# Sinkhorn attention and a two-layer feed-forward: four more groups of batch 0 compute their scores twice, with a new instruction order

## The chip, the cores and the metric

The kernel runs on one core of one Trainium2 chip. The time is the device time of an execution in microseconds (us); where several executions were timed, the median is given. Within the core, five engines work side by side, each through its own list of instructions in order: PE (TensorE, the matrix multiplier, with its weight loads shown as PEld), DVE (VectorE), ACT (ScalarE), POOL (GpSimd) and SP (SyncE, which here only starts transfers). PE writes to PSUM, eight banks; DVE and ACT read it from there.

## The reference

q, k, v are (4, 8, 768, 64): batch, head, token, feature. The 768 tokens of a head are 8 blocks of 96.

```
P = sort_net                                   # (4, 8, 8, 8)
for _ in range(5):
    P = exp(P - max(P, -1)); P /= sum(P, -1) + 1e-9; P /= sum(P, -2) + 1e-9
k_sorted = einsum('bhij,bhjcd->bhicd', P, k_blocks);  v_sorted likewise
scores = q_block @ k_sorted_block.T / sqrt(64)          # 96 x 96 inside each block
attn = exp(scores - max(scores, -1)); attn /= sum(attn, -1) + 1e-9
x = (attn @ v_sorted), heads side by side               # 3072 tokens x 512
h = x @ w_in                                            # 512 -> 2048
g = max(h, 0) + alpha * min(h, 0)
out = g @ w_out                                         # 2048 -> 512, f32
```

The scale 1/8 is folded into the matrix that sorts the keys.

## The kernel before

The whole computation is written as a list of 1158 operations, each with what it reads and writes. A table `ORDER` then gives, engine by engine, the order in which the operations stand; a number such as `480` is an operation, and `4.2` means four filler matmuls (128x512, line 1006) into bank 2, whose result nobody reads. A second table, `BANKS`, gives the PSUM banks. `emit` adds a semaphore wait wherever an operation needs another engine's result. So the two tables alone set the order of the work; nothing is decided at run time, and an engine whose next instruction has to wait holds back everything behind it.

The work has these parts:

- The Sinkhorn loop on 32x64 numbers (lines 546 to 560), DVE and ACT in turn. It ends with `Pb`, which is spread (`spread0`, line 569) into the sorting matrices `BDK` and `BDV`. Meanwhile PE runs 226 tiny matmuls (line 899) and 12 fillers (line 1006), which need `identb` (an identity that ACT copies from `identf`).
- Preparation of each batch. q is transposed (batch 0 on PE, line 434, and copied out to `QT`; later batches by conversion to `QI` and a transposing transfer). Keys are sorted by matmul (line 634 for batch 0, line 656 later, from `KSz`, which POOL or DVE fill at line 644) and copied to `KT`. Values are first rearranged within `VST` by copies on POOL, ACT or DVE, then sorted (lines 680, 701) and copied out to `VS`. Most of these copies go through one helper, line 395.
- Attention in 32 groups, group g being block g % 8 of batch g // 8, all 8 heads at once. A string `STYLE`, one letter to a group, chooses how the exponentials get to be laid out with keys on the partitions, as the next product needs them:
  - all styles: 8 matmuls for the scores with queries on the partitions (line 736) and a DVE reduction for minus the row maxima, to `nf` in f32 or `nm` in bf16 (line 740);
  - `t`: ACT takes the exponential in 8 instructions, one to a head, the maximum as bias (`Esb`, line 764); PE transposes it (8 matmuls, line 775); ACT or DVE copies the result to `ET` (line 395);
  - `f`: the same 8 instructions, and a transposing transfer from `Esb` to `ET` on SP's queue (line 784);
  - `n`: PE computes the scores again, this time with keys on the partitions (8 matmuls, line 748), then adds minus the maxima of each query by 8 matmuls of the broadcast `nm` with the identity (line 756), and ACT takes the exponential of all 768 columns in one instruction straight to `ET` (line 790).
  
  The product with the values (line 800), the division by the row sums (`rec`, `xq`, lines 806, 809) and the transposition to `xT` (line 823 on PE for groups 0 to 13, line 816 on SP later) are common to all.
- The feed-forward, in 9 chunks of groups (`CHUNKS`: groups 0-1, 2-3, then four at a time). First layer: line 844 on PE, relu(-h) to `t` on ACT (line 851), and `hT` on DVE (line 855). Second layer: line 877, 128 tokens at a time, in four parts of four matmuls each; parts 0 and 1 read the first half of `w_out_bf`, parts 2 and 3 the second. Its result is copied to `outstg` and stored by SP.

All loads go through POOL's queue; a half of `w_out_bf` is loaded by each of the two instructions at line 931, a batch's q by line 417, its keys by line 467, its values by line 477.

The lines that choose between the styles, in `attention`:

```
nx, nk_ = (nf[m], ("nf", m)) if st != "n" else (nm[m], ("nm", m))
...
else:
    G.add(PE, s2, 175, r=kt_keys + qt_keys + [("nm", m)], w=[X], prio=prio + 0.04, mode=2)
    G.add(PE, sub, 8 * 43, r=[("nm", m), "identb"], w=[X], prio=prio + 0.04)
    G.add(ACT, lambda e: e.activation(
        AP(ET[me], 0, [[800, 96], [384, 2], [1, 384]]),
        AP(ps, X.at(), [[LP, 96], [X.step, 2], [1, 384]]),
        ACTF.Exp), 810, r=[X], w=[("ET", me)], prio=prio + 0.05)
```

Of the kernel before, what the change touches and what calls it, by code (L numbers as in the profile page):

```python
# [29 lines left out]
LP_K = {1: 4.6, 2: 9, 3: 16}  # L30
LP_V = {0: 0.5, 1: 4.8, 2: 12, 3: 12.1}
PRQ = {1: 6, 2: 13, 3: 20}
STYLE = 'nntttttt' + 'f' * 24
XPE = range(14)
NWI = 2
CHUNKS = [(0, 2), (2, 4), (4, 8), (8, 12), (12, 16), (16, 20), (20, 24), (24, 28), (28, 32)]
# [3 lines left out]

ORDER = {
    "pool": """
# [3 lines left out]
        635 636 681 680 639 638 683 637 682 792 737 823 643 736 822 645 641""",  # L46
    "sync": """
        0 5 144 146 142 339 386 401 436 381 377 379 468 268 495 529 566 598 644 649 675 623 365 570 705 602 729 562
        519 759 679 642 701 653 665 787 709 640 733 817 841 791 869 777 763 895 921 821 845 873 746 941 856 813 967
        1019 945 925 954 899 993 917 885 983 1039 997 971 1052 1023 1043 1015 1073 1118 1097 1157 1139 1145 1151""",  # L50
    "pe": """
# [14 lines left out]
        1094 1116 1119 1152 1135 1140 1128 1125 1136 1095 1141 1137 1142 1153 1154 1155 1146 1143 1147 1148 1149""",  # L66
    "act": """
# [8 lines left out]
        1078 1075 1081 1087 1084 1099 1102 1108 1123 1132 1090 1105 1117 1120 1111 1126 1129 1096 1150""",  # L76
    "dve": """
# [13 lines left out]
        1091 1106 1121 1112 1130 1127 1156 1138 1144""",  # L91
}
BANKS = (
    "0620452304660313015574545676716120235015223234367260175607327340012372454015406160154561306612014745"
    "2372547711223545052501562444232357714015607641707623454050002063014560754074271564560372340127266560"
    "1352511234767505012321670645230525760101427573401234475010153772230155166122341043423245312323046000"
    "15625371235600260123354164151324667144620334051605"
)


# [218 lines left out]
def bass_sinkhorn_attn__then__act_prelu_kernel(  # L319
# [393 lines left out]
    def attention(g, prio):  # L713
        b, i = g // NB, g % NB
        n, m, me = b % 2, g % 2, g % NE
        st = STYLE[g]
        kt_keys = [("KT", n, u) for u in range(6)]
# [328 lines left out]
```

## Time and profile before

| | |
|---|---|
| median of 3 runs | 238.45 us (237.95 to 238.58) |
| the profiled execution | 237.39 us, of which the profile's span is 235.7 us |
| PE busy | 221.9 us (94%) |
| DVE, ACT, POOL busy | 174.8 us (74%), 156.5 us (66%), 82.8 us (35%) |
| moved by transfers | 29.17 MB, mean 124 GB/s |

The profiled execution is 1.06 us below the median; 1.69 us of it lie outside the span. Times in the profile's views count from the span's start. A busy PE includes the time in which a matmul runs through the array, so short gaps between matmuls do not show as idle.

### The profile page before, as it was taken

Reading aid. Unit: us, or ns where it says so; the run is one execution under the profiler, and the core shown is the slowest. Engines: PE = TensorE matmul, PEld = TensorE weight load, DVE = VectorE, ACT = ScalarE, POOL = GpSimd, SP = SyncE. Lnnn points to the kernel's source line nnn. Section 1 sums busy time; section 2 is a strip of 40 time slices with the busy share of each in tenths; the row PEclk is TensorE's granted clock in tenths of the full one; section 3 lists DMA queues with packets and bytes.
Section 4 is the critical chain, followed back from the end, with each engine's and each line's share of the span. In section 5 each row is a group of like instructions: output and inputs, shape, how many; then the busy total and the mean of one; then the engine's idle time right before and its main releaser. Section 6 shows DMA issues by size and latency. Waiting matters only on the chain.

```text
span 235.7 us, 5903 instructions
## 1 busy us (share of the span) xinstructions
PE 221.9 (94%) x2345; PEld 136.6 (58%) x2370; DVE 174.8 (74%) x364; ACT 156.5 (66%) x445; POOL 82.8 (35%) x107
## 2 busy tenths in 40 slices
PE   3969988999999999999999999999999999999995
PEld 3367767887456565566455655655555555555553
DVE  3739999998989997989778776786864557575412
ACT  3278999967999978987778658775752344062420
POOL 7947999673876695600303710000000000000000
PEclk9979999999999999999999999999999999999999
DMA  5999999999989998547066633134415122411113
GB/s 83 219 226 195 212 203 208 175 187 207 162 137 177 171 180 132 105 83 170 17 162 167 128 67 95 34 69 109 112 35 118 54 92 50 101 41 45 45 46 134
DMA packets 47307, 29.17 MB, mean 124 GB/s; under 512 B 37024, under 2 KB 42416, under 8 KB 47152
## 3 DMA queue, kind: packets, MB, share of 16 engines
q0 software_dynamic: 7408, 13.63, 33.0%
q1 hardware_dynamic: 39872, 15.16, 29.8%
q8 instruction: 18, 0.29, 0.5%
q14 instruction: 9, 0.07, 0.1%
HBM read 27.28 MB, written 6.29 MB: 142 GB/s over the span
## 4 chain that ended last, share of the span: by engine, by line
PE 74%; ACT 11%; DVE 9%; DMA 2%; POOL 2%; issue 1%; SPq 0%; POOLq 0%; ACTq 0%
PE ps L877 30%; PE ps L844 29%; ACT Esb L764 6%; PE ps L800 3%; PE ps L736 3%; DVE hT L855 2%; PE ps L680 2%; DMA ET<-Esb 2%; ACT VS L395 1%; DVE nf L740 1%; PE ps L656 1%; ACT KT L395 1%; PE ps L701 1%; PE ps L823 1%; PE ps L434 1%
## 5 line engine op out<-in xcount | busy, mean ns | idle before, releaser
L855 DVE SCALAR_TENSOR_TENSOR hT<-t,omaT,ps 128x384 bf16<-128x384 f32 (+1 forms) x144 | 76.8, 561 | 33.2 <-ACT t L851 32.4
L844 PE MATMUL ps<-xT,w_in_bf 128*128 128x384 bf16 (+1 forms) x576 | 96.9, 308 | 1.0 <-DVE hT L855 0.7
L851 ACT ACTIVATE t<-ps 128x384 f32<-128x384 f32 x128 | 59.4, 498 | 48.2 <-PE ps L844 30.5
L877 PE MATMUL ps<-w_out_bf,hT 128*128 128x512 bf16 (+1 forms) x375 | 89.2, 370 | 1.9 <-issue 0.6
L844 PEld LDWEIGHTS ps<-xT,w_in_bf 128*128 128x128 bf16 x576 | 51.5, 98 | 32.7 <-DVE hT L855 2.4
L764 ACT ACTIVATE Esb<-ps,nf 96x96 bf16<-96x96 f32 x240 | 57.9, 356 | 4.1 <-DVE nf L740 3.3
L877 PEld LDWEIGHTS ps<-w_out_bf,hT 128*128 128x128 bf16 x400 | 37.0, 98 | 33.1 <-DVE hT L855 0.2
L740 DVE TENSOR_REDUCE nf<-ps 96x8 f32<-96x768 f32 x30 | 28.1, 946 | 4.3 <-PE ps L736 3.1
L395 POOL COPY VST<-VST 64x384 bf16<-64x384 bf16 (+1 forms) x28 | 23.8, 852 | 6.0 <-DMA VST<-in_v_dram 4.7
L809 DVE TENSOR_TENSOR xq<-ps,rec 96x512 bf16<-96x512 f32 x32 | 21.7, 681 | 0.6
L644 POOL COPY KSz<-KS 64x512 bf16<-64x512 bf16 x27 | 16.5, 612 | 13.3 <-PE ps L656 11.6
L395 POOL COPY QT<-QS 128x1024 bf16<-128x1024 bf16 x7 | 13.8, 1965 | 17.7 <-DMA QS<-QI 17.5
L800 PEld LDWEIGHTS ps<-VS,ET 96*128 96x128 bf16 x256 | 11.3, 98 | 4.5 <-ACT Esb L764 0.5
L800 PE MATMUL ps<-VS,ET 96*128 96x65 bf16 x256 | 13.1, 194 | 0.3 <-ACT ET L790 0.3
L395 ACT ACTIVATE outstg<-ps 128x512 f32<-128x512 f32 (+1 forms) x12 | 7.0, 586 | 9.3 <-PE ps L877 9.3
L395 DVE CAST VS<-ps 96x512 bf16<-96x512 f32 x17 | 12.4, 746 | 0.1
L736 PEld LDWEIGHTS ps<-KT,QT 64*96 64x96 bf16 x256 | 7.8, 121 | 7.9 <-DVE hT L855 1.5
L736 PE MATMUL ps<-KT,QT 64*96 64x96 bf16 x256 | 10.6, 211 | 1.4 <-DVE xT L395 1.2
L395 ACT ACTIVATE KT<-ps 128x512 bf16<-128x512 f32 x16 | 9.5, 610 | 3.4 <-PE ps L656 2.4
L395 DVE COPY outstg<-ps 128x512 f32<-128x512 f32 (+1 forms) x13 | 8.5, 661 | 4.2 <-PE ps L877 4.2
L395 ACT ACTIVATE VS<-ps 96x512 bf16<-96x512 f32 x15 | 10.9, 747 | 0.6 <-PE ps L701 0.6
L395 POOL COPY QI<-QS 128x1024 bf16<-128x1024 bf16 x8 | 8.3, 1037 | 6.1 <-DMA QS<-in_q_dram 4.1
(101 smaller groups left out, 164.7 us busy)
## 6 DMA issues: line engine op xcount, KB each, us to landing
out_dram<-outstg SPq DMA_DIRECT2D x23, 256.0 KB, 2.3
KS<-in_k_dram POOLq DMA_DIRECT2D x6, 384.0 KB, 10.5
w_in_bf<-in_moe_w_in_dram POOLq DMA_DIRECT2D x2, 1024.0 KB, 20.8
w_out_bf<-in_moe_w_out_dram POOLq DMA_DIRECT2D x2, 1024.0 KB, 19.8
QS<-in_q_dram POOLq DMA_DIRECT2D x2, 768.0 KB, 10.5
VST<-in_v_dram POOLq DMA_DIRECT2D x2, 768.0 KB, 11.4
VST<-in_v_dram POOLq DMA_DIRECT2D x4, 384.0 KB, 9.0
QS<-in_q_dram POOLq DMA_DIRECT2D x4, 384.0 KB, 6.1
```

What stands on the lines that cost most here:

```text
L395: return e.activation(o, i, ACTF.Copy) if e is nc.scalar else e.tensor_copy(o, i)
L644: G.add(("pool", "dve"), lambda e, hp=hp: e.tensor_copy(AP(KSz, hp * 64 * 3072 + u % 3 * 1024 + hp * 64, [[3072, 64], [128, 8], [1, 64]]), ...
L680: inst = e.matmul(AP(ps, T.at(d % 8 * 64), [[LP, 128], [1, 64]]), st, AP(BDV, b * 64, [[128, 64 + 64 * b], [1, 64]]))
L736: inst = e.matmul(sc(h4, hp), qs(h4, hp), ks(h4, hp))
L740: G.add(DVE, lambda e: e.tensor_reduce(AP(nx, 0, [[8, 96], [4, 2], [1, 4]]), AP(ps, X.at(), [[LP, 96], [X.step, 2], [96, 4], [1, 96]]), Ax ...
L764: inst = e.activation(AP(Esb[me], p * 128, [[1024, 96], [1, 96]]), AP(ps, X.at((p % 4) * 96) + p // 4 * X.step, [[LP, 96], [1, 96]]), ACTF ...
L800: inst = e.matmul(AP(ps, Z.at(h4 * 68) + hp * Z.step, [[LP, 128], [1, 65]]), AP(ET[me], (hp * 4 + h4) * 96, [[800, 96], [1, 128]]), AP(VS, ...
L809: G.add(DVE, lambda e: e.tensor_tensor(out=AP(xq[me], 0, [[512, 96], [256, 2], [64, 4], [1, 64]]), in0=AP(ps, Z.at(), [[LP, 96], [Z.step, ...
L844: inst = e.matmul(AP(ps, T.at(x * n), [[LP, 128], [1, n]]), AP(w_in_bf, kt * DFF + (ft + x) * 128, [[KT_TILES * DFF, 128], [1, 128]]), AP( ...
L851: G.add(ACT, lambda e: e.activation(AP(t1[tb], 0, [[384, 128], [1, w * n]]), AP(ps, T.at(), [[LP, 128], [1, w * n]]), ACTF.Relu, scale=-1. ...
L855: G.add(DVE, lambda e, x=x: e.scalar_tensor_tensor(out=AP(hT, (ft + x) * RING + tok % RING, [[FT_TILES * RING, 128], [1, n]]), in0=AP(t1[t ...
L877: inst = e.matmul(AP(ps, T.at(), [[LP, 128], [1, n]]), AP(hT, ft * RING + tok % RING, [[FT_TILES * RING, 128], [1, 128]]), AP(w_out_bf, ft ...
```

## The change

`STYLE` goes from two `n` and six `t` for batch 0 to six `n` and two `t`; the other 24 groups stay `f`. `ORDER` and `BANKS` are replaced as a whole; fillers go from 24 to 23 matmuls. No function is edited. (The new file is two lines longer, so line 736 before is line 738 after, and so on.)

```
-STYLE = 'nntttttt' + 'f' * 24
+STYLE = 'nnnnnntt'+'f'*24
...
     "pe": """
-        2 4.1 4.2 4.3 90 124 73 129 88 110 86 96 98 92 102 100 94 118 112 104 2.5 180 148 2.0 2.3 106 108 158 150
...
+        2 124 2.0 4.2 1.3 4.4 1.5 88 73 129 90 112 86 98 100 94 102 96 92 4.2 108 104 106 148 4.5 1.5 116 114 158
...
```

Counted over the whole program, these instructions differ in number or in engine:

| | before | after |
|---|---|---|
| PE: scores a second time (line 748), maxima (line 756) | 16, 16 | 48, 48 |
| PE: transposes of `Esb` (line 775) | 48 | 16 |
| ACT: exponentials by head (line 764), whole (line 790) | 240, 2 | 208, 6 |
| copies to `ET` (line 395), ACT and DVE | 2 and 4 | 0 and 2 |
| `KSz` copies (line 644), DVE and POOL | 9 and 27 | 2 and 34 |
| `VST` copies, batches 0 and 1: POOL, ACT, DVE | 18, 4, 0 | 11, 10, 1 |
| `VST` copies, batches 2 and 3: POOL, ACT, DVE | 10, 4, 2 | 10, 6, 0 |
| copies to `VS`, ACT and DVE | 15 and 17 | 18 and 14 |
| copies to `KT`, ACT and DVE | 16 and 8 | 14 and 10 |
| `QT` of later batches, POOL, ACT, DVE | 7, 1, 1 | 8, 0, 1 |

PE from the second group's scores to the first matmuls of the feed-forward. Before:

```order
L748 MATMUL ps<-QT0,KT0 96x96 x8
L756 MATMUL ps<-identb,nm1 96x96 x8
L775 MATMUL ps<-identb,Esb2 96x96 x8
L800 MATMUL ps<-VS,ET0 128x65 x8
L800 MATMUL ps<-VS,ET1 128x65 x8
L1006 MATMUL ps<-identb 128x512 x4
L736 MATMUL ps<-KT0,QT0 96x96 x8
L823 MATMUL ps<-identb,xq0 128x96 x4
L775 MATMUL ps<-identb,Esb0 96x96 x8
L823 MATMUL ps<-identb,xq1 128x96 x4
L736 MATMUL ps<-KT0,QT0 96x96 x8
L844 MATMUL ps<-xT,w_in_bf 128x192 x8
```

The same stretch after:

```order
L758 MATMUL ps<-identb,nm1 96x96 x8
L1008 MATMUL ps<-identb 128x512
L802 MATMUL ps<-VS,ET0 128x65 x8
L802 MATMUL ps<-VS,ET1 128x65 x8
L750 MATMUL ps<-QT0,KT0 96x96 x8
L738 MATMUL ps<-KT0,QT0 96x96 x8
L758 MATMUL ps<-identb,nm0 96x96 x8
L825 MATMUL ps<-identb,xq0 128x96 x4
L825 MATMUL ps<-identb,xq1 128x96 x4
L682 MATMUL ps<-BDV,VST 128x64 x8
L658 MATMUL ps<-BDM,KSz 128x64 x8
L846 MATMUL ps<-xT,w_in_bf 128x192 x8
```

Transposes of `Esb` for groups 2 and 3 and the scores of group 5 are gone from it; the third group's second scores and maxima stand there now, with fewer fillers.

DVE in the same place, from the products' row sums of groups 0 and 1 to their columns of `xT`. Before:

```order
L806 RECIPROCAL rec1<-ps 96x8
L809 TENSOR_TENSOR xq0<-ps,rec0 96x512
L809 TENSOR_TENSOR xq1<-ps,rec1 96x512
L740 TENSOR_REDUCE nf0<-ps 96x8
L616 TENSOR_TENSOR BDV<-mkhV,dsel 64x64
L395 COPY xT<-ps 128x4x96 x2
```

After:

```order
L808 RECIPROCAL rec1<-ps 96x8
L811 TENSOR_TENSOR xq0<-ps,rec0 96x512
L811 TENSOR_TENSOR xq1<-ps,rec1 96x512
L397 COPY xT<-ps 128x4x96 x2
L742 TENSOR_REDUCE nm1<-ps 96x8
```

The row maxima of a later group and `BDV` no longer stand ahead of the two copies to `xT`.

POOL's loads around `w_out_bf`. Before (the first of the two loads of `w_out_bf` follows the loads of `w_in_bf` at once):

```order
L926 DMA w_in_bf<-in_moe_w_in_dram 128x4x1024 x2
L931 DMA w_out_bf<-in_moe_w_out_dram 128x8x512
L395 COPY VST<-VST 64x384 x2
L467 DMA KS0<-in_k_dram 128x2x768
L395 COPY VST<-VST 64x384
```

After, the piece that ends with that same load:

```order
L469 DMA KS0<-in_k_dram 128x2x768
L397 COPY VST<-VST 64x384 x3
L646 COPY KSz<-KS1 64x8x64
L397 COPY VST<-VST 64x384
L646 COPY KSz<-KS1 64x8x64
L503 MEMSET Esb1 96x8x32
L646 COPY KSz<-KS1 64x8x64
L397 COPY VST<-VST 64x384 x2
L646 COPY KSz<-KS1 64x8x64 x2
L916 MEMSET VST 64x192
L646 COPY KSz<-KS1 64x8x64 x2
L933 DMA w_out_bf<-in_moe_w_out_dram 128x8x512
```

The load of batch 1's q moved up, to just behind `w_in_bf` and one copy ahead of this piece, and the first half of `w_out_bf` moved down, behind seven `VST` and seven `KSz` copies in all. The second half of `w_out_bf` stands in both behind the loads of batches 2 and 3's values, ten rows after the first half in this one.

At the start, PE's transposition of alpha (line 936) moved from behind the 12 fillers to ahead of them, and on ACT `identb`, which the fillers need, moved from behind the first Sinkhorn exponential to behind the second and behind `mkK`.

More of the change, by code (lines that the diff above doesn't have):

```diff
@@ L42 @@
     "pool": """
[3 rows of a table removed]
-        635 636 681 680 639 638 683 637 682 792 737 823 643 736 822 645 641""",
[3 rows of a table added]
+        713 712 822 635 681 737 736 823 636 793 792 637 638 639 641 643 645""",
     "sync": """
-        0 5 144 146 142 339 386 401 436 381 377 379 468 268 495 529 566 598 644 649 675 623 365 570 705 602 729 562
-        519 759 679 642 701 653 665 787 709 640 733 817 841 791 869 777 763 895 921 821 845 873 746 941 856 813 967
-        1019 945 925 954 899 993 917 885 983 1039 997 971 1052 1023 1043 1015 1073 1118 1097 1157 1139 1145 1151""",
+        0 5 142 144 146 386 401 268 339 436 379 377 468 381 495 529 598 562 566 649 602 705 570 675 365 729 653 644
+        519 640 642 679 623 709 759 787 733 817 701 665 869 841 763 895 791 921 845 821 941 813 967 856 746 777 899
+        925 873 993 885 954 1019 945 1039 971 1023 997 917 1043 983 1073 1015 1097 1052 1118 1145 1157 1139 1151""",
     "pe": """
[14 rows of a table removed]
-        1094 1116 1119 1152 1135 1140 1128 1125 1136 1095 1141 1137 1142 1153 1154 1155 1146 1143 1147 1148 1149""",
-    "act": """
[8 rows of a table removed]
-        1078 1075 1081 1087 1084 1099 1102 1108 1123 1132 1090 1105 1117 1120 1111 1126 1129 1096 1150""",
-    "dve": """
[13 rows of a table removed]
-        1091 1106 1121 1112 1130 1127 1156 1138 1144""",
[15 rows of a table added]
+        1137 1146 1147 1148 1149""",
+    "act": """
[9 rows of a table added]
+        1138 1150""",
+    "dve": """
[13 rows of a table added]
+        1130 1117 1156""",
 }
 BANKS = (
[L94 to L97, printed above, removed]
+    "0706163521434537252106723010123453454734670142552013467673010152350160127647334445566555340115120160"
+    "1402767232647215016727136723344676723047574465012377677267642301460402554170123446412367703050167521"
+    "4501124074652334020700013437615623230011012237761013445707002345532414523046745237645023231065023234"
+    "6357451225252323170346160044437523320531147263"
 )
```

76 rows, old and new, of the table ORDER are left out of this document.

## The prediction

> **What bounds the kernel now.** I read the page's first lines first, then each engine's busy time by stage, then the chain that ended last and its waits, then the groups by form.
>
> ```profile
> span 235.7 us, 5903 instructions
> PE 221.9 (94%) x2345; PEld 136.6 (58%) x2370; DVE 174.8 (74%) x364; ACT 156.5 (66%) x445; POOL 82.8 (35%) x107
> ```
> ```profile
> 0.00:20.00 20.00, 14.27 (x422) 10.09 (x423) 11.17 (x54) 9.66 (x19) 13.29 (x26) 0.91 0.90 177
> 20.00:30.00 10.00, 9.71 (x164) 7.43 (x163) 9.60 (x19) 9.52 (x26) 9.37 (x13) 1.00 1.08 208
> 30.00:50.00 20.00, 17.86 (x318) 15.73 (x316) 19.27 (x46) 19.21 (x58) 16.94 (x24) 1.00 1.12 193
> 50.00:80.00 30.00, 28.75 (x272) 18.17 (x274) 28.52 (x56) 25.58 (x64) 20.84 (x25) 1.00 1.08 174
> 80.00:100.00 20.00, 19.70 (x212) 11.40 (x213) 18.24 (x34) 16.95 (x60) 12.94 (x14) 1.00 0.91 142
> 100.00:236.00 136.00, 131.62 (x972) 73.81 (x988) 88.01 (x160) 75.60 (x224) 9.47 (x9) 1.00 0.35 85
> ```
>
> Each row of the second fence is a stretch and its length, then busy time of PE, PEld, DVE, ACT and POOL, the granted PE clock, the share of the transfer engines and GB/s. From 80 us on PE is all but full, so what is left of the 235.7 us after that is PE's own list. Between 20 and 80 us nearly everything is full: DVE is idle for only 0.40 + 0.73 + 1.48 = 2.6 of 60 us, ACT for 0.48 + 0.79 + 4.4 = 5.7, and PE waits for these two: 0.29 + 2.14 + 1.25 us, and 0.30 more up to 100 us, together 3.98 us. Ahead of 20 us PE is idle for 5.7 us, the Sinkhorn loop. The time can therefore be kept as an account: PE's work plus PE's idle time. The chain shows who makes PE wait in the 30s:
>
> ```profile
> 26.79 0.81 ACT ET L790
> 27.60 1.83 ACT Esb L764 x8
> ...
> 33.49 1.95 ACT Esb L764 x8
> ...
> 36.45 1.94 ACT Esb L764 x8
> ```
>
> ACT's exponentials by head, about 1.94 us for a group, follow each other; one exponential of a whole group takes 0.81 us (the first row).
>
> **The change, part by part.** Four groups change from eight exponentials to one, and DVE and ACT's copies to `ET` go from six to two. Rows of the groups by form:
>
> ```profile
> L790 ACT ACTIVATE ET<-ps 96x768 bf16<-96x768 f32 x2 | 1.6, 807 | 0.1
> L395 DVE COPY ET<-ps 96x768 bf16<-96x768 bf16 x4 | 2.2, 543 | 0.1
> L395 ACT ACTIVATE ET<-ps 96x768 bf16<-96x768 bf16 x2 | 1.6, 806 | 0.0
> L644 DVE COPY KSz<-KS 64x512 bf16<-64x512 bf16 x9 | 4.5, 496 | 0.2
> L644 POOL COPY KSz<-KS 64x512 bf16<-64x512 bf16 x27 | 16.5, 612 | 13.3 <-PE ps L656 11.6
> L395 POOL COPY VST<-VST 64x384 bf16<-64x384 bf16 x18 | 15.0, 836 | 0.9
> L395 ACT ACTIVATE VST<-VST 64x384 bf16<-64x384 bf16 x4 | 3.3, 856 | 0.3 <-DMA VST<-in_v_dram 0.3
> L395 DVE CAST VS<-ps 96x512 bf16<-96x512 f32 x17 | 12.4, 746 | 0.1
> ```
>
> ACT saves 4 x (1.94 - 0.81) = 4.5 us on exponentials and 2 x 0.81 = 1.6 us on copies. The new order spends nearly all of this on six more `VST` copies of batch 1 (6 x 0.86 = 5.1 us) taken from POOL, so ACT gains little before 50 us. POOL in turn takes seven `KSz` copies (7 x 0.61 = 4.3 us) and gives up seven `VST` copies (7 x 0.84 = 5.9 us). DVE is the one that is relieved: two `ET` copies (1.1 us), seven `KSz` copies (7 x 0.50 = 3.5 us), three `VS` copies (2.2 us), against two `KT` and a `VST` copy more (about 1.9 us): some 5 us less by 100 us. Nothing is charged for POOL's longer stretches: in the 50s it is idle much of the time, 9.2 of 30 us.
>
> PE pays. The chain gives blocks of its small matmuls:
>
> ```profile
> 14.25 0.99 PE ps L434 x16
> ...
> 16.11 0.99 PE ps L434 x16
> 17.10 1.01 PE ps L634 x48
> ...
> 21.46 0.49 PE ps L736 x16
> 21.95 0.97 PE ps L1006 x4
> ...
> 24.84 0.49 PE ps L756 x8
> ```
> ```profile
> 26.59 0.52 PE L775 MATMUL ps<-identb,Esb 96*96 96x96 bf16 x8
> 26.95 0.41 PE L800 MATMUL ps<-VS,ET 96*128 96x65 bf16 x8
> ...
> 31.37 0.38 PE L736 MATMUL ps<-KT,QT 64*96 64x96 bf16 x8 [1.16 <-DVE xT L395]
> 31.68 0.83 PE L844 MATMUL ps<-xT,w_in_bf 128*128 128x192 bf16 x8
> ```
>
> Eight second scores take as long as eight first ones, 0.49 / 2 = 0.25 us; the maxima 0.49 us; the eight transposes dropped 26.95 - 26.59 = 0.36 us. That is 0.38 us more for a group, 1.5 us for four. One filler less is 0.97 / 4 = 0.24 us. PE's work: +1.3 us.
>
> PE's idle time is where it can come back. The largest single wait is the 1.16 us in the row at 31.37, and the rows there say why: DVE did a row maximum and `BDV` ahead of the two `xT` copies. In the new order these two copies come first, so the first feed-forward matmul can start some 0.9 to 1.5 us sooner after the products of groups 0 and 1. I also compared DVE's list from the first row maximum to the last `ET` copy of batch 0, in the old order this stretch:
>
> ```profile
> 21.81:49.47 27.66, 25.22 (x446) 21.28 (x441) 26.71 (x59) 26.41 (x78) 24.09 (x33) 1.00 1.11 197
> ```
>
> DVE (the third of the busy times) is busy for 26.71 of 27.66 us. Both orders have put 18 pieces of `hT` behind them at its end, and the new one has 0.9 to 1.6 us less work in it (the `ET` copies, `dsel`, which moves into idle time ahead, and one `KSz` copy at 0.3 to 1.0 us, against one `VST` copy and one `xT` copy). Past 50 us DVE has three to four us less, but PE can only use its own 1.25 + 0.30 us of waits. If no wait of the 3.98 us were left, the account would give -4.0 + 1.3 = -2.7 us; if all were left or returned elsewhere, +1.3 us. A new order does not remove every wait. I take 2.5 of the 3.98 us, nearer to the full removal since DVE's relief (5 us) is larger than all of them: -2.5 + 1.3 = -1.2 us.
>
> The start changes too. `identb` now waits for the second Sinkhorn round's exponential and for `mkK`, and the 12 fillers wait for it; on DVE a 32x512 memset comes into the loop. I put `Pb` 0.35 us later (an estimate: between 0, if it falls into the gaps in which DVE waits for ACT, and 0.5 us, its length as the same memset has it on POOL). On the other side stands the clock:
>
> ```profile
> 10.40:13.87 3.47, 1.69 (x30) 0.89 (x29) 2.60 (x14) 2.26 (x6) 1.04 (x2) 1.00 0.91 182
> 13.87:17.28 3.41, 3.41 (x65) 3.09 (x64) 0.66 (x6) 2.67 (x3) 2.56 (x3) 0.54 1.09 229
> ```
> ```profile
> 11.03 0.64 PE L434 MATMUL ps<-identb,QS 128*64 128x128 bf16 x16
> 11.60 0.23 PE L936 MATMUL ps<-identf,alphaR 16*128 16x16 f32 x1
> ```
> ```profile
> 5.08 0.31 ACT L395 ACTIVATE identb<-identf 128x128 bf16<-128x128 f32 x1 [1.84 <-POOL identf L486]
> ```
>
> After a stretch with PE busy for 1.69 of 3.47 us the clock was halved for 3.4 us, just while the queries are transposed and the keys sorted, which lie on the chain. With `identb` and the fillers behind it some 2 us later, PE works nearly up to `Pb`, and that half-clock stretch may not come. The blocks at 14.25 and 16.11 would then take 11.60 - 11.03 = 0.57 us each, as the same block did before the clock fell, so 0.84 us less for the two; the sorting is little faster, since its keys land only about then. I put 0.9 us on it, and nothing below (0 if the clock is halved all the same). The Trainium skill, TensorE: Matmul & The Clock Gate, Part 1, says that the clock is halved after an idle window of about 3.4 us, that a busy one releases it, and that the window runs freely. The length agrees with the two rows; half-busy counted as idle here, which the page does not say. By the free-running window alone the start would differ from execution to execution, and the sum would be anywhere between the two results below.
>
> Sum for the likeliest case: PE's work +1.3, waits -2.5, `Pb` +0.35, clock -0.9: -1.75 us. The profiled execution of 237.39 us would take 235.6. The median of the runs shown lies 1.06 us higher; the same difference gives 238.45 - 1.75 = 236.7 us.
>
> **The first half of `w_out_bf`** moves behind 14 copies on POOL, which take 7 x 0.84 + 7 x 0.61 = 10.2 us from about 19 us on, and a wait for a free `KSz`: from 14.3 to an issue between 30 and 34 us. The transfer engines are full throughout, batch 1's q goes ahead of it, and it is needed at about 50 us (the first row of the second fence below). I cost it at nothing; the cover is the 16 us or more up to then, against 14.7 to 24.9 us from issue to landing in the rows here; if that cover is gone, PE waits at its first block of line 877, but with the queue's same total ahead of it I expect the landing near 44 us. The second half decides more, see the third rival.
>
> ```profile
> L931 POOL DMA_DIRECT2D w_out_bf<-in_moe_w_out_dram x2: 889/894/898, 14.3 to 47.0; - x2
> DMA to landing us min/median/max: 14.7/19.8/24.9
> ```
> ```profile
> 51.17 0.81 PE L877 MATMUL ps<-w_out_bf,hT 128*128 128x512 bf16 x3
> ...
> 63.21 1.03 PE L877 MATMUL ps<-w_out_bf,hT 128*128 128x512 bf16 x4
> ```
>
> **The rivals.**
>
> *Half clock at the start again.* If PE's gap before `Pb` still counts, the 0.9 us is not saved: -0.85 us, 237.6 us. For it: with a warm clock the fillers end sooner and leave a gap. Against it: the gap is then about 2 us of 3.4, at the limit. The page named above would have this case whenever the window's edge falls badly.
>
> *The waits only move.* PE is given 1.5 us more work, all between 22 and 45 us, where ACT has been handed five us of `VST` copies; of the 6.1 us that it saves, 5.1 are spent again, so its last exponential of batch 0 hardly comes earlier. If only 1.3 of the 3.98 us go, the account is 0; with +0.35 and half of the clock's 0.9 us, 238.3 us, no change.
>
> *Slower: the second half of `w_out_bf` comes late.* In the old order it is issued at 47.0 us and, if the shorter time is its own, lands at 61.7; the first matmul that needs it is the fifth block of line 877, at 63.21 us, so 1.5 us of cover. In the new order it stands behind the first half's late issue, a conversion of q, four value loads and eight small POOL pieces; by POOL's rows I get an issue at about 49.3 us. PE would want it at about 62.5. If the queue is still full at 49 us, the landing stays at about 61.5 and nothing happens; if it is issued into an empty queue, it lands at 64.0 or later, PE stands still for 1.5 us or more, behind it all later blocks, and DVE and ACT run into full `hT` and PSUM. It decides from a landing at about 65 us, where 2.5 us of waiting use up all that is gained: 239.3 us with some 0.8 us more lost. For it: POOL has no idle time in the 20s and 30s to make good a delay. Against: the transfer engines are busy throughout that stage (share 1.08 to 1.12).
>
> *More.* If every wait to 100 us goes and the clock holds, -4.0 + 1.3 + 0.35 - 0.9 = -3.2 us: 235.2 us.
>
> **Chances.** Likeliest (236.7) 0.42; half clock (237.6) 0.18; waits move (238.3) 0.16; late weights or another order fault of that size (239.3) 0.16; more (235.2) 0.08. About 0.3%, 0.7 us, is what a measurement of this kernel can tell from no change: 237.75 to 239.15 is "same". Faster: the first and last and most of the half-clock case, 0.61; same: the rest of that, and the moved waits but for a little, 0.22; slower: 0.17. The range reaches from a little below the fifth case to the middle of the fourth: 235.0 to 239.2 us. The likeliest case's own range is 236.0 to 237.4.
>
> **What would show it.** Right: the first matmul of the feed-forward at 29.5 to 30.7 us instead of 31.68; PE idle 20 to 100 us at about 1.5 us instead of 3.98; no exponential by head on the chain before 30 us; a granted clock of 0.9 or more from 13.9 to 17.3 us; PE's last matmul about 1.7 us sooner. DVE's busy time about 4 to 5 us lower in all, with ACT's about the same. The order past 100 us leaves PE as full as before, 131.6 us or a little more of the rest. Wrong: a wait of a block of line 877 for the load of `w_out_bf` near 63 us; a wait of PE for `xT` or `hT` of about 1 us at another place; PE idle beyond 100 us by more than the 4.4 us of before; a start where `Pb` comes more than 0.5 us late.

## The result and the profile after

| | time, us | ratio to the kernel before (95%) |
|---|---|---|
| before, 4 runs beside it | 238.51 (237.95 to 239.72) | |
| the changed kernel, 4 runs | 236.45 (235.15 to 236.96) | 0.989 [0.9865, 0.9916] |
| predicted | 236.7 (235.0 to 239.2) | |

The ratios in this document leave out executions more than 1.5% above the fastest of the same kernel; medians and counts of clocks have all.

The profiled execution of the changed kernel took 236.34 us, 1.05 us less than the one of before (237.39). Its page starts, and its stages read (columns as in the prediction):

```profile
span 234.6 us, 5953 instructions
PE 222.9 (95%) x2401; PEld 137.5 (59%) x2401; DVE 172.7 (74%) x356; ACT 154.6 (66%) x422; POOL 81.8 (35%) x106
```
```profile
0.00:20.00 20.00, 13.76 (x421) 9.40 (x422) 13.62 (x59) 10.63 (x21) 11.87 (x22) 1.00 0.88 177
20.00:30.00 10.00, 9.31 (x177) 7.77 (x177) 8.45 (x18) 8.79 (x12) 7.13 (x11) 1.00 1.09 211
30.00:50.00 20.00, 19.41 (x344) 16.86 (x342) 19.06 (x46) 17.23 (x43) 15.06 (x24) 1.00 1.14 201
50.00:80.00 30.00, 28.52 (x258) 17.13 (x256) 27.40 (x48) 24.38 (x65) 24.23 (x28) 1.00 1.04 173
80.00:100.00 20.00, 19.99 (x229) 12.43 (x228) 18.49 (x34) 18.27 (x64) 8.94 (x8) 1.00 0.68 108
...
10.40:13.87 3.47, 3.26 (x24) 1.33 (x22) 2.72 (x14) 2.71 (x5) 0.00 (x0) 1.00 1.08 214
13.87:17.28 3.41, 3.41 (x115) 3.13 (x113) 2.87 (x8) 1.45 (x3) 0.48 (x1) 1.00 1.10 231
```

PE's idle time from 20 to 50 us fell from 2.43 to 0.69 + 0.59 = 1.28 us, from 80 to 100 us from 0.30 to 0.01; but from 50 to 80 us it rose from 1.25 to 1.48. The last two rows show the clock: no half-clock stretch, and PE busy for 3.26 us of the 3.47 where it was 1.69. PE's list at the places that the prediction named:

```profile
8.40 4.69 PE L1008 MATMUL ps<-identb 128*128 128x512 bf16 x12
13.31 0.64 PE L436 MATMUL ps<-identb,QS 128*64 128x128 bf16 x16 [0.21 <-DMA QS<-in_q_dram]
13.88 0.37 PE L571 MATMUL ps<-Pb,w_out_bf 32*128 32x8 bf16 x8
...
29.66 0.83 PE L846 MATMUL ps<-xT,w_in_bf 128*128 128x192 bf16 x8
...
63.00 1.03 PE L879 MATMUL ps<-w_out_bf,hT 128*128 128x512 bf16 x4
...
68.34 0.38 PE L738 MATMUL ps<-KT,QT 64*96 64x96 bf16 x8 [0.85 <-DVE hT L857]
```

The feed-forward starts at 29.66 us instead of 31.68, and the fifth block of the second layer, the one at 63.00 us, did not wait for weights. New is the wait of 0.85 us at 68.34, put down to `hT`. DVE's list and POOL's, a little earlier, say what held `hT` up:

```profile
63.78 3.98 DVE L397 COPY QT<-QS 128x1024 bf16<-128x1024 bf16 x1
```
```profile
61.56 1.98 POOL L397 COPY QT<-QS 128x1024 bf16<-128x1024 bf16 x1 [0.60 <-DMA QS<-QI]
63.49 1.40 POOL L469 DMA_DIRECT2D KS<-in_k_dram  x2
64.89 1.95 POOL L397 COPY QT<-QS 128x1024 bf16<-128x1024 bf16 x1
```

DVE's copy of `QT` took 3.98 us; in the kernel before the same copy started at 65.5 us and took 1.02:

```profile
L395 DVE COPY QT<-QS x1: 1024/1024/1024, 65.5 to 65.5; 128x1024 bf16<-128x1024 bf16 x1
```

The long one ended 0.92 us after POOL's second copy (64.89 + 1.95 = 66.84), as if it had only then begun.

### The profile page after: what moved, and what is told of

Read it like the earlier page. It is cut to its first block, busy times and chain, and to the rows that moved or that the text cites. A ratio compares the mean times of both kernels' runs of the same rounds, so it can differ in the third digit from the quotient of the medians.

```text
span 234.6 us, 5953 instructions
## 1 busy us (share of the span) xinstructions
PE 222.9 (95%) x2401; PEld 137.5 (59%) x2401; DVE 172.7 (74%) x356; ACT 154.6 (66%) x422; POOL 81.8 (35%) x106
## 3 DMA queue, kind: packets, MB, share of 16 engines
q0 software_dynamic: 7408, 13.63, 33.2%
## 4 chain that ended last, share of the span: by engine, by line
PE 82%; DVE 6%; DMA 5%; ACT 5%; issue 1%; POOL 0%; POOLq 0%
PE ps L879 34%; PE ps L846 32%; DMA QS<-in_q_dram 5%; PE ps L802 3%; PE ps L738 3%; PE ps L682 2%; DVE hT L857 2%; DVE QT L397 2%; ACT t L853 2%; PE ps L703 1%; PE ps L658 1%; ACT VST L397 1%; PE ps L1008 1%; ACT ET L792 1%; PE ps L825 1%
## 5 line engine op out<-in xcount | busy, mean ns | idle before, releaser
L879 PE MATMUL ps<-w_out_bf,hT 128*128 128x512 bf16 (+1 forms) x400 | 93.7, 371 | 0.4 <-DVE hT L857 0.3
L766 ACT ACTIVATE Esb<-ps,nf 96x96 bf16<-96x96 f32 x208 | 49.7, 353 | 8.2 <-DVE nf L742 8.1
L742 DVE TENSOR_REDUCE nf<-ps 96x8 f32<-96x768 f32 x26 | 24.5, 946 | 2.5 <-PE ps L738 2.3
L646 POOL COPY KSz<-KS 64x512 bf16<-64x512 bf16 x34 | 20.7, 610 | 15.6 <-PE ps L658 11.5
L397 POOL COPY QT<-QS 128x1024 bf16<-128x1024 bf16 x8 | 15.7, 1964 | 12.9 <-DMA QS<-QI 12.7
L397 POOL COPY VST<-VST 64x384 bf16<-64x384 bf16 (+1 forms) x21 | 18.1, 863 | 1.9 <-DMA VST<-in_v_dram 0.9
L397 ACT ACTIVATE outstg<-ps 128x512 f32<-128x512 f32 (+1 forms) x12 | 7.1, 590 | 11.6 <-PE ps L879 11.6
L397 ACT ACTIVATE VS<-ps 96x512 bf16<-96x512 f32 x18 | 13.0, 747 | 1.6 <-PE ps L703 0.9
L802 PEld LDWEIGHTS ps<-VS,ET 96*128 96x128 bf16 x256 | 11.3, 98 | 4.2 <-ACT ET L792 0.6
L397 ACT ACTIVATE VST<-VST 64x384 bf16<-64x384 bf16 (+1 forms) x16 | 13.5, 870 | 0.4 <-DMA VST<-in_v_dram 0.3
L738 PE MATMUL ps<-KT,QT 64*96 64x96 bf16 x256 | 11.2, 212 | 1.1 <-DVE hT L857 0.9
L397 DVE COPY outstg<-ps 128x512 f32<-128x512 f32 (+1 forms) x13 | 8.6, 662 | 4.8 <-PE ps L879 4.8
L738 PEld LDWEIGHTS ps<-KT,QT 64*96 64x96 bf16 x256 | 8.1, 121 | 6.2 <-DVE hT L857 2.5
L808 DVE RECIPROCAL rec<-ps 96x8 f32<-96x8 f32 x32 | 6.4, 200 | 6.0 <-PE ps L802 5.6
L397 DVE CAST VS<-ps 96x512 bf16<-96x512 f32 x14 | 10.4, 742 | 0.3
```

The costliest lines, as they stand in the source:

```text
L397: return e.activation(o, i, ACTF.Copy) if e is nc.scalar else e.tensor_copy(o, i)
L646: G.add(("pool", "dve"), lambda e, hp=hp: e.tensor_copy(AP(KSz, hp * 64 * 3072 + u % 3 * 1024 + hp * 64, [[3072, 64], [128, 8], [1, 64]]), ...
L738: inst = e.matmul(sc(h4, hp), qs(h4, hp), ks(h4, hp))
L742: G.add(DVE, lambda e: e.tensor_reduce(AP(nx, 0, [[8, 96], [4, 2], [1, 4]]), AP(ps, X.at(), [[LP, 96], [X.step, 2], [96, 4], [1, 96]]), Ax ...
L766: inst = e.activation(AP(Esb[me], p * 128, [[1024, 96], [1, 96]]), AP(ps, X.at((p % 4) * 96) + p // 4 * X.step, [[LP, 96], [1, 96]]), ACTF ...
L802: inst = e.matmul(AP(ps, Z.at(h4 * 68) + hp * Z.step, [[LP, 128], [1, 65]]), AP(ET[me], (hp * 4 + h4) * 96, [[800, 96], [1, 128]]), AP(VS, ...
```

## The experiments

All in one table; under it, each with its edit. They were timed in three sets, each with runs of the kernel before beside it, and a ratio holds within its set: the four kernels from "changed, again" to "row maximum first"; then early `identb`, seven groups, three groups changed and late `identb`; then late alpha, `xT` first and both moves. The clock is the granted clock of a whole execution, with the number of executions. A stretch of 3.4 us at half clock in some 236 us makes 0.007.

| kernel | median, us | ratio (95%) | clock |
|---|---|---|---|
| before, 63 runs beside the rest, medians of the three sets | 238.64 to 238.89 | | 0.993 x17, 0.986 x39, 0.978 x7 |
| changed, again | 235.63 | 0.987 [0.9832, 0.9907] | 1.000 x6 |
| changed, QT exchange | 234.99 | 0.9849 [0.9813, 0.9885] | 1.000 x6 |
| changed, all QT on POOL | 237.88 | 0.9959 [0.9924, 0.9995] | 1.000 x6, 0.993 x6 |
| changed, row maximum first | 236.82 | 0.9924 [0.9894, 0.9955] | 1.000 x9, 0.993 x3 |
| changed, early `identb` | 235.55 | 0.9879 [0.9848, 0.9911] | 1.000 x6 |
| changed, early `identb`, late alpha | 245.47 | 1.0263 [1.0208, 1.0317] | 0.972 x4, 0.979 x2 |
| changed, QT exchange, seven groups | 235.96 | 0.9892 [0.9868, 0.9916] | 1.000 x6 |
| before, three groups changed | 248.83 | 1.0425 [1.0396, 1.0455] | 0.952 to 0.972 x6 |
| before, late `identb` | 237.42 | 0.9946 [0.9921, 0.997] | 1.000 x12 |
| before, `xT` first | 238.39 | 0.9991 [0.9963, 1.002] | 0.993 x6, 0.986 x6 |
| before, both moves | 238.01 | 0.996 [0.993, 0.999] | 1.000 x10, 0.979 x2 |

(0.999 is counted with 1.000, 0.991 and 0.992 with 0.993, 0.984 and 0.985 with 0.986, 0.977 and 0.979 with 0.978.)

**The changed kernel again.** No edit.

> The changed kernel once more, as the baseline of this set of runs. Every theory: 0.989 of the time before, 236.1 to 236.8 us where the kernel before takes 238.5, and in the trace the same DVE copy of QT of about 4 us near 64 us with PE's idle time from 50 to 80 us near 1.5 us.

The time came out 0.8 us lower than in the first set and below the range expected, and the long copy was not there: in this execution DVE's copy began at the end of POOL's first copy, 0.11 us into POOL's issuing of two loads, took 1.07 us, and that issuing took 2.02 us instead of 1.40. PE's idle time from 50 to 80 us was 0.68 us, not 1.48.

```profile
64.16 1.07 DVE L397 COPY QT<-QS 128x1024 bf16<-128x1024 bf16 x1
```
```profile
62.11 2.00 POOL L397 COPY QT<-QS 128x1024 bf16<-128x1024 bf16 x1 [1.41 <-DMA QS<-QI]
64.05 2.02 POOL L469 DMA_DIRECT2D KS<-in_k_dram  x2
66.06 1.97 POOL L397 COPY QT<-QS 128x1024 bf16<-128x1024 bf16 x1
```

So the expectation of the same 4 us was wrong: in the profile shown first the copy came up 0.29 us into the issuing, and which of the two engines goes first differs between executions of one kernel.

**The QT exchange.** ACT does the third `QT` copy (operation 147) in place of two `VST` copies, POOL these two:

```
-act:  610 504 463 506 484 540
+act:  610 147 463 484 540
-pool: 634 633 147 368
+pool: 634 633 504 506 368
```

> The changed kernel with one exchange near 64 us: ACT does the third copy of QT for batch 1 in place of two VST copies, POOL does these two in its place; DVE's own copy of QT stays where it is. Theory (a POOL copy running at the same time blocks DVE's copy, and that cost 0.7 us of the change's gain): DVE's copy of QT takes 1.0 to 1.2 us instead of 3.98 if POOL's copies alone block it; PE's wait of 0.85 us for hT at 68 us goes; 0.4 to 0.8 us less than the changed kernel, 235.7 to 236.0 us. Sub-case: POOL's issuing of loads blocks it too (63.5 to 64.9 us): about 2 us, then 0.2 to 0.5 us less. Rival (the copy is long by itself in this place, or PE's wait has another cause): the copy stays near 4 us, or the time is within 0.2 us of the changed kernel, since ACT's 2.0 us copy holds up t in turn.

```profile
63.11 2.05 DVE L397 COPY QT<-QS 128x1024 bf16<-128x1024 bf16 x1
```
```profile
62.31 1.94 POOL L397 COPY QT<-QS 128x1024 bf16<-128x1024 bf16 x1 [1.07 <-DMA QS<-QI]
64.20 1.81 POOL L469 DMA_DIRECT2D KS<-in_k_dram  x2
```
```profile
50.00:80.00 30.00, 29.49 (x273) 17.75 (x270) 26.24 (x51) 26.21 (x69) 24.11 (x29) 1.00 1.06 178
```

DVE's copy reached its turn while POOL's ran and ended 0.91 us after it (64.25). The length expected, 1.0 to 1.2 us, was missed for that reason. The difference in time was as expected: 0.50 us by the means below the changed kernel beside it (234.99 and 235.49, six runs each), 0.64 us by the medians. But the theory is not shown by it: in the profile of the changed kernel beside it the copy took 1.07 us, half of what it takes here, and PE's idle time from 50 to 80 us is 0.51 us here and 0.68 there. Where the rest of the 0.5 us comes from is open. It has the lowest median here.

**All QT copies on POOL.** `145` from DVE to POOL, behind `147`.

> The changed kernel with DVE's copy of QT given to POOL, behind POOL's own two. DVE does not copy QT at all. Theory (DVE was held up for 3 us, hT behind it): hT comes 4 us sooner, PE's wait for hT at 68 us goes, but the last QT comes 1 us later than before (68.8 instead of 67.8 us), so PE waits for QT instead, 0.3 to 0.6 us: 0 to 0.5 us less than the changed kernel. Rival (it was QT that PE waited for at 68 us, the wait only being put down to hT): PE's wait grows by 1 us and the time by 0.5 to 1.0 us.

The time went the rival's way and further: PE now waits 1.4 us for `QT` (`PE ps L738 <- POOL QT L397`), and in the executions at full clock the mean is 236.66 us, 1.2 us above the changed kernel; in six of twelve a half-clock stretch came as well, and they took 238.94 us on average. The rival's reason does not hold for the profile shown first: there the last `QT` ended at 67.76 us, `hT` behind it at 68.29, and PE went on at 68.34. Here the third copy ended at 69.33 us, and PE went on at 69.48. So the theory had the right wait and put it too small: three copies one after the other are late.

**The row maximum first.** On DVE the fourth group's maximum (`209`) goes back ahead of the `xT` copies (`157 167`).

```
-dve: 155 165 157 167 209 177
+dve: 155 165 209 157 167 177
```

> The changed kernel with the fourth group's row maximum put back ahead of the two xT copies on DVE, one instruction moved past two pieces. Theory of the prediction (the earlier xT copies are what brings the first feed-forward block from 31.68 to 29.66 us and about half of what the waits give back): the first feed-forward block comes 0.8 to 1.0 us later, near 30.6 us, PE's idle time from 20 to 50 us rises from 1.3 to 1.9 to 2.3 us and the time by 0.4 to 0.9 us. Rival (PE has other work ready, and the lead that is lost at 30 us comes back or is eaten by the later wait at 68 us anyway): within 0.3 us of the changed kernel.

PE's list, and PE by 2 us, in the profiled execution (239.06 us, one of three with clock 0.993):

```profile
30.03 0.61 PE L682 MATMUL ps<-BDV,VST 128*128 128x64 bf16 x8 [0.79 <-DVE xT L397]
...
30.88 1.47 PE L846 MATMUL ps<-xT,w_in_bf 128*128 128x192 bf16 x8
```
```profile
28.00:30.00 2.00, 0.99 (x16) 0.70 (x15) 2.00 (x5) 1.96 (x3) 1.50 (x3) 0.96 1.12 211
30.00:32.00 2.00, 1.97 (x24) 1.88 (x25) 0.93 (x2) 1.10 (x2) 0.81 (x2) 0.50 1.13 215
```

The theory held: PE waits 0.79 us for `xT`, and at full clock the time is about 0.9 us above the changed kernel (mean 236.43 against 235.49). What it did not foresee: in the profiled execution the clock is halved behind the wait (0.83 us for the block became 1.47). Three of the twelve have a clock of 0.993, as one such stretch gives, and take 238.5 us on average; where it lies in the other two was not profiled.

**Three groups changed in the old order.** `STYLE` is `nnnnnttt`, the new matmuls stand where the transposes were or a little earlier, the exponential at the first possible place on ACT; everything else is the kernel before.

```
-STYLE = 'nntttttt' + 'f' * 24
+STYLE = 'nnnnnttt' + 'f' * 24
 pe:  182 183 to ahead of 116; 210 ahead of 211; 242 ahead of 243
 act: 182 210 242 out; 184 to ahead of 117; 244 to behind 205
 dve: 184 244 out; 181 to behind 159
```

> The kernel before, in its own order, with three of the four groups changed (third, fourth and fifth compute their scores twice; the sixth stays as it was, since its ET buffer comes free too late in that order). Second scores and maxima go where the transposes were or a little earlier, the exponential of a whole group to where ACT had eight; nothing else moves. By the account: PE's work +1.15 us (3 x 0.38). Theory (the gain is the new order and the clock at the start, not the computation): the early half-clock stretches stay, granted clock 0.979 to 0.993 as before; ACT's 5 us and DVE's 1.1 us of relief take back 0.5 to 1.5 us of PE's waits; the time is between 0.4 us below and 0.7 us above the kernel before. Rival (the computation itself is the gain, the order only a way to it): PE idle from 20 to 100 us falls from 3.98 to about 1.5 us, time 1.2 to 2 us below the kernel before.

```profile
20.00:30.00 10.00, 8.19 (x133) 6.55 (x133) 6.05 (x11) 5.48 (x9) 9.39 (x14) 0.96 1.08 209
30.00:50.00 20.00, 17.16 (x249) 13.04 (x247) 15.05 (x32) 12.20 (x32) 11.26 (x16) 0.76 0.90 158
```

Both expectations missed by far: 10 us slower. PE is idle for 4.65 us from 20 to 50 us, in pieces between 0.2 and 0.9 us, and the granted clock is 0.76 over 20 us. The computation by itself, put into a list that was written for other durations, makes PE wait for maxima and exponentials that stand behind other work. (Another placing by hand could do better; only this one was tried.)

**Late `identb` in the kernel before.** One ACT instruction moved:

```
-act: 38 10 45 52 59
+act: 38 45 52 10 59
```

> The kernel before with one ACT instruction moved: the copy to identb behind the third exponential of the Sinkhorn loop instead of behind the first, so that the fillers run up to Pb. Theory (an early half-clock stretch costs nearly 1 us, and the kernel before has one at 13.9 to 17.3 us in every execution): the granted clock of the whole run rises by 0.007 (0.986 to 0.993 for most), no half clock at 13.9 to 17.3 us, time 0.7 to 1.0 us below the kernel before. Rival (the Sinkhorn loop and the loads set the start, the half clock is hidden beside them): time within 0.3 us of before. Rival (it only comes later): clock 0.986 as before, the halved stretch near 30 us, time the same or up to 0.5 us more.

```profile
10.40:13.87 3.47, 3.47 (x14) 1.20 (x14) 2.60 (x14) 2.56 (x6) 1.04 (x2) 1.00 0.91 181
13.87:17.28 3.41, 3.41 (x90) 3.10 (x88) 0.60 (x6) 1.79 (x3) 2.00 (x3) 1.00 1.07 223
```

1.3 us less (0.7 to 1.9), more than expected, since not one half-clock stretch but all of them went, in all 12 executions.

**The kernel before again, for a second profile.** No edit.

> The kernel before, once more, for a second profile of it. In the runs of it beside the others the granted clock was 0.993, 0.986 or 0.978 (237.95, 238.88 and 239.64 us on average), as if one, two or three stretches of 3.4 us were halved; the profiled execution shown first had 0.993 and one. Theory (a second one falls where PE waits for xT): with a clock of 0.986 a second half-clock stretch between 27 and 36 us. Rival: it falls somewhere else, or the clock is a little lower everywhere.

```profile
10.40:13.87 3.47, 2.15 (x30) 1.13 (x29) 2.60 (x14) 2.56 (x6) 1.04 (x2) 1.00 0.96 191
13.87:17.28 3.41, 3.41 (x83) 3.17 (x81) 1.10 (x6) 2.35 (x3) 2.54 (x3) 0.69 1.09 227
27.50:31.00 3.50, 2.55 (x36) 1.59 (x36) 3.40 (x8) 3.46 (x10) 3.24 (x5) 1.00 1.11 210
31.00:34.40 3.40, 2.90 (x32) 2.28 (x32) 2.73 (x7) 3.18 (x14) 3.23 (x5) 0.68 1.14 190
34.40:38.00 3.60, 3.60 (x49) 3.33 (x48) 3.51 (x9) 2.57 (x11) 3.35 (x5) 0.82 1.24 207
```

This execution (238.19 us, clock 0.986) shows the second stretch where the theory had it: behind PE's wait for `xT`, from about 32 us. The first one lasts from 15.2 to 18.6 us, against 14.2 to 17.6 in the profile shown first, so it starts 1.0 us later. By the Trainium skill, TensorE: Matmul & The Clock Gate, Part 1, the window that the clock is set by runs freely, so the moment of the change differs from run to run; the two profiles agree.

**`xT` first, and both moves, in the kernel before.**

```
-dve: 155 165 241 136 157 167 168
+dve: 155 165 157 167 241 136 168
```

> The kernel before with two DVE instructions moved: the two xT copies of the first groups ahead of the fifth group's row maximum and BDV. Theory (PE's wait of 1.16 us in the 20s and 30s is for these copies, and PE half idle there is what halves the clock a second time): first feed-forward block at 30.2 to 30.7 us instead of 31.68, clock 0.993 for most runs instead of 0.986, 0.8 to 1.8 us below the kernel before. Rival (the fifth group's exponentials, which wait for that maximum, are late in turn): within 0.4 us of before, clock unchanged.

> The kernel before with these two and the identb copy moved, three instructions in all; the computation of every group stays as it was. Theory (most of the change's gain is the clock and the xT wait, not the scores computed twice): clock 1.000, 1.9 to 2.7 us below the kernel before, 0.989 to 0.992, as the whole change. Rival (the computation and the rest of the order carry half of it): as the identb copy alone, 0.994 to 0.996.

Both theories fell. PE's waits with `xT` first (total us, times, longest):

```profile
PE ps L775 <- ACT Esb L764: 0.8, 1, 0.8
PE ps L844 <- DVE hT L855: 0.7, 2, 0.5
PE ps L844 <- DVE xT L395: 0.7, 1, 0.7
```

The feed-forward starts at 31.08 us instead of 31.68 or, in the second profile, 31.81, but the exponentials by head, which need the maximum that now comes later, are late for the transposes: 0.8 us. The waits only moved, and PE's idle time from 20 to 50 us is 0.29 + 2.41 us, as before. Both moves together do no better than `identb` alone (means at full clock 237.78 and 237.56 us), and two of the twelve executions have a clock of 0.979 again.

**Early `identb` in the changed kernel; then late alpha too.** The ACT move above backwards (`10` behind `38`); the second kernel also moves PE's transposition of alpha (`124`) behind the fillers and the first block of queries.

> The changed kernel with the same instruction moved the other way: identb's copy behind the first exponential. Theory: the fillers run early, PE is half idle ahead of Pb, a half-clock stretch of 3.4 us returns; clock 0.993 instead of 1.000 and 0.7 to 1.0 us more than the changed kernel, 236.4 to 237.2 us. Rival (hidden): within 0.3 us of the changed kernel. Rival (in the new order PE is busy enough ahead of Pb by other work): clock 1.000, no change.

> The changed kernel with identb's copy behind the first exponential, and on PE the transpose of alphaR behind the fillers and the first block of queries, where it stood in the order before. With identb alone moved nothing changed, since PE stood at that transpose until 8.5 us. Theory (the half clock comes from PE standing still ahead of Pb): fillers from 6 to 11 us, PE busy for less than 2 us of the 3.47 from 10.4 us, half clock near 14 to 17 us in every execution, clock 0.993, 0.7 to 1.2 us more than the changed kernel, 236.5 to 237.0 us. Rival (hidden by the loads of that time): within 0.3 us of the changed kernel.

PE's list of the first, then of the second:

```profile
8.33 0.21 PE L901 MATMUL ps<-bz 32*32 32x32 bf16 x3 [5.15 <-issue]
8.68 4.65 PE L1008 MATMUL ps<-identb 128*128 128x512 bf16 x12
```
```profile
8.06 0.21 PE L901 MATMUL ps<-bz 32*32 32x32 bf16 x3 [4.89 <-issue]
8.21 5.02 PE L1008 MATMUL ps<-identb 128*128 128x512 bf16 x12
```

The first changed nothing: the fillers started at 8.68 us all the same, though `identb` was ready at 5.51 us. In the second the transposition of alpha stands behind the fillers, and they still started only at 8.21 us. So neither holds them. PE stands still for about 5 us ahead of the last 3 of the 226 tiny matmuls, and the profile names nothing that it waits for ("issue"). This gap is in every profile: it ends between 5.33 and 5.88 us in the old order and between 7.51 and 8.33 us in the new one. What makes it longer there is not shown.

The second kernel is no test of the clock: PE waited 5.1 us for `Pb`, until 19.34 us (13.88 in the changed kernel), since DVE's copy of the transposed alpha (`125`) stands in the middle of the Sinkhorn loop in the new order, which I had not seen; PE then stood still, with three to four half-clock stretches. It shows only what a late `Pb` costs: 5.5 us at the start became 9.8 us.

**Seven groups.** On top of the QT exchange the seventh group as the first six (`310 311` on PE ahead of `282`, `312` on ACT in place of `310`).

> The exchange of the QT copies that gave 0.985 of the time before, and the seventh group of batch 0 in the manner of the first six; the order is otherwise kept. By the account: PE's work +0.38 us, ACT -1.1 us, DVE -0.5 us near 45 us. Theory (PE is full from 30 to 50 us, 0.6 us of waits left, so no wait is there to pay for a further group): 0.2 to 0.5 us more than with the exchange alone, 235.2 to 235.5 us. Rival (ACT and DVE still set the pace there): 0.3 to 0.6 us less.

```profile
PE ps L802 <- ACT ET L792: 1.2, 2, 0.9
```

0.9892 of the time before against 0.9849 with the exchange alone, measured in another set and with intervals that overlap: 0.7 to 1 us more. Of it 0.4 us is the work of the account. The new wait of 0.9 us for the exponential does not explain the rest: PE's idle time from 20 to 100 us is 2.03 us in this profile and 2.07 with the exchange alone, so other waits went; PE is busy for 0.8 us longer (223.6 and 222.8). No gain from a further group was measured; its price is open.

## Why the prediction was right, point by point

**PE's work, +1.3 us: right.** The three groups of matmuls in the second profile of before, then in the changed kernel:

```profile
L775 PE MATMUL ps<-identb,Esb 96*96 96x96 bf16 x48 | 3.5, 222 | 0.0
L756 PE MATMUL ps<-identb,nm 96*96 96x96 bf16 x16 | 1.1, 212 | 0.0
L748 PE MATMUL ps<-QT,KT 64*96 64x96 bf16 x16 | 0.8, 206 | 0.0
```
```profile
L758 PE MATMUL ps<-identb,nm 96*96 96x96 bf16 x48 | 3.3, 211 | 0.0
L750 PE MATMUL ps<-QT,KT 64*96 64x96 bf16 x48 | 2.3, 211 | 0.0
L777 PE MATMUL ps<-identb,Esb 96*96 96x96 bf16 x16 | 1.1, 209 | 0.0
```

6.7 against 5.4 us, and one filler of 0.24 us less: +1.1 us. In the first profile of before, where none of them fell into a half-clock stretch, the three rows add up to 5.1 us, which gives +1.4.

**PE's waits, -2.5 us: too large.** From 3.98 us from 20 to 100 us, 2.77 were left in the profiled execution: -1.2 us. In the profile of the changed kernel again, 1.96 were left: -2.0. And a part of the 3.98 was no waiting. The first profile of before lacks the records of 25 of the second layer's 400 matmuls; its row of them, then that of the second profile:

```profile
L877 PE MATMUL ps<-w_out_bf,hT 128*128 128x512 bf16 (+1 forms) x375 | 89.2, 370 | 1.9 <-issue 0.6
```
```profile
L877 PE MATMUL ps<-w_out_bf,hT 128*128 128x512 bf16 (+1 forms) x400 | 94.1, 371 | 0.0
```

A missing record looks like idle time: the figure behind the last bar, the idle time ahead of these matmuls, is 1.9 us in the one and 0.0 in the other. The second profile, with all of them, has 3.18 us from 20 to 100 us (2.40 of them up to 50, as in the first), and 2.9 us of idle time past 100 us where the first has 4.1. From 3.18 us the change is -0.4 or -1.2. So in every pairing the 2.5 us were too many. The waits of the 20s and 30s went as described, and putting the maximum back gave 0.9 us of it back; 0.8 us of the term failed at 64 us, where DVE's `QT` copy beside POOL's copies took 3 us more than its row of before; the account had charged nothing for POOL's longer stretches. One sign of being wrong did come: a wait of PE for `hT` of about 1 us at another place, the 0.85 us at 68.34.

**`Pb`, +0.35 us: not there.** `Pb` ended where it had; the new limit at 13.3 us is the load of q, which the row of 13.31 shows.

**The clock, -0.9 us: right in kind, too small, and with the wrong instruction.** The stretch at 13.87 us did not come. But the profiled execution of before was one with a single half-clock stretch, and most executions have two: 17 of 63 at 0.993 took 238.10 us on average, 39 at 0.986 238.81, 7 at 0.978 239.93, so 0.7 to 1.1 us each. I carried the 1.06 us by which the median lay above the profile over as a constant. A part of it is a second stretch, which the change removes too; the larger part is that the profiled execution was a quick one, 0.71 us below the average of those with a single stretch. The changed kernel's profiled execution lies only 0.11 us below its median. And it is not `identb` that makes the fillers late in the new order, since moving it back changed nothing, but PE's gap ahead of them, which the prediction did not look at.

So the sum was right by two errors that cancel: for the profiled execution 235.6 us was forecast and 236.34 came, and for the distance to the median 1.06 us was carried over and 0.11 came. That the median was met within 0.3 us is luck to that extent.

**The rivals.** Half clock again: in none of the changed kernel's executions. The waits only move: this is what `xT` first does in the old order, not the whole change. The second half of `w_out_bf`: the two loads were issued at 33.2 and 49.0 us and landed 11.3 to 12.2 us later, so by 61.2 us:

```profile
L933 POOL DMA_DIRECT2D w_out_bf<-in_moe_w_out_dram x2: 884/891/898, 33.2 to 49.0; - x2
DMA to landing us min/median/max: 11.3/11.7/12.2
```

The block at 63.00 us did not wait.

**Where the gain comes from.** Late `identb` took the half-clock stretches out of the kernel before and gave 0.9946 of its time; the whole change gives 0.987 to 0.989. Within one set, the means are 238.87 us for the kernel before, 237.56 with late `identb`, and 235.82 for the changed kernel with early `identb`, the latter two at full clock throughout. So about two fifths of the 3.1 us go with the clock; by the interval of the first step, 0.7 to 1.9 us, it can be a quarter or more than half. The rest is what the new order and the computation bring at full clock, and they were not separated: the computation alone, as it was placed here, costs 10 us, the `xT` order alone gives nothing, and taking the latter out of the changed kernel costs 0.9 us, but the whole new order with the old computation was not run.

Open: why the kernel before with late `identb` keeps the full clock in all 12 executions, though its PE is busy for only 2.55 of the 3.5 us from 27.5 us on, as in the execution above where the clock was halved behind it; what makes PE's gap among the tiny matmuls longer in the new order; and where the half-clock stretch falls with all `QT` copies on POOL.

## What to carry to other kernels

Look at the granted clock of every execution before trusting one profile: here the profiled one had one half-clock stretch and most others had two, and that difference was part of the gain. A wait of the bounding engine can cost its length and then a slower clock, so a short gap ahead of dense work is worth more than its row says. A step that relieves an engine and the order that uses the relief have to be priced together: of the parts that were tried alone here, one gave nothing and one a loss. And count the records before taking idle time for waiting: 25 missing matmuls made part of the account's stock of waits.

## What was not expected of the hardware

DVE's copy of 128x1024 bf16 takes 1.02 to 1.07 us by itself. When it came up during a POOL copy it ended 0.91 us after that one (2.05 us with the QT exchange, 2.13 us with the row maximum first). When it came up 0.29 us into POOL's issuing of two loads, it ended only after the issuing and the copy behind it, 3.98 us (and 4.07 us in the kernel with early `identb`, where it came up 0.22 us into them). When it came up 0.11 us into them, in the changed kernel again, it took 1.07 us and POOL's issuing 2.02 instead of 1.40 us. The Trainium skill, SBUF — State Buffer, SBUF: two separate sides, says that some DVE operations and a GpSimd operation take a shared pair of ports for a whole instruction, whoever starts first, and that the other stands still; the rows agree, and add that DVE can stand through an issuing and the copy behind it. What decides who is first is not settled: in the kernel with seven groups the copy came up 0.78 us into the issuing of the same two loads and took 1.18 us, while the issuing took 2.10.
